# Lower words of the weights as integers into VectorE's product, their scale in the addition

## Chip, core and metric

One Trainium2 chip, of which the kernel uses one core. The time is device microseconds (us) of one launch. It was run three times: 1009.37, 1009.37 and 1008.32 us, median 1009.37. The names below: PE is TensorE (matmul), PEld its weight load, DVE is VectorE, ACT is ScalarE, POOL is GpSimd, SP is SyncE, which issues nearly all DMAs.

## What is computed

The reference is an attention with exponential features, whose result goes through a two-layer network with a cosine gate:

```python
def phi(x):                                   # x: (8, 8, 576, 64), w_phi: (64, 128)
    proj = np.einsum('bhsd,df->bhsf', x, w_phi)
    proj = proj - np.max(np.abs(proj), axis=-1, keepdims=True)
    return np.concatenate([np.exp(proj), np.exp(-proj)], axis=-1)
q_p, k_p = phi(q), phi(k)
kv = np.einsum('bhsf,bhsd->bhfd', k_p, v)
z = np.sum(k_p, axis=2)
num = np.einsum('bhsf,bhfd->bhsd', q_p, kv)
den = np.einsum('bhsf,bhf->bhs', q_p, z)[..., None] + 1e-06
x = num / den                                 # as 4608 tokens x 512
h = x @ w_in                                  # w_in: 512 x 2048
out = (h * np.cos(h)) @ w_out                 # w_out: 2048 x 512
```

`w_in` and `w_out` are drawn in 64-bit floats, and the kernel gets them as 64-bit words. For TensorE it splits each weight into two 32-bit floats, a high part and a remainder.

## The kernel before

**Two streams of work.** 32 units of attention (a unit is two heads of one batch) produce x, transposed, in a DRAM buffer `xs`; the network works on it in chunks of 512 tokens, in visits that take some of the eight pairs of w_in and w_out tiles each. The two streams run interleaved: attention ends near 680 us, and the network goes on to the end.

**Order.** Every piece of work is a `Step` with an engine, a function, the steps it depends on and the buffers it takes. `ORDER` (L88) is a list of all step numbers written out by hand; `plan()` (L260) follows it as it stands, and each engine runs its own steps in that order, one after the other. The costs given to a `Step` (0.4, 2.05, ...) are not used in placing anything. Waits between engines are derived from who reads and writes which buffer: a buffer is written anew when the last reader of its old contents is done.

**Weights.** `convert` (L368) is called for 16 tiles, w_in and w_out in turn (wi0, wo0, wi1, wo1, ...). Each loads 1 MB of 64-bit words into `w_raw`, of which there is one buffer (`w_raw=1` in `rings`, L285), so that the next tile's load has to wait until this one's last reader is done; the eight `f_raw` loads of `fold` (L501) use the same buffer afterwards. The scratch tiles `w_t0`, `w_t1`, `w_t2` exist once too. Per tile, `low` and `top` are the lower and upper 32-bit words, read with a step of 8 bytes (L386), and then:
- `scale`, ScalarE: L390 makes t0 from `top`; L391 converts `low` from unsigned integers into floats times 2^-52, in t2.
- `bits`, VectorE: L396, then L399 (reads `top`), then L402, which leaves in t1 the upper bits as a float and in t0 its power of two.
- `rest`, VectorE, L421: t2 = t2 x t0.
- `add`, VectorE, L435 (w_in) or L437 (w_out): the sum with t2. `high` (ScalarE, L50) and `low` (VectorE, L55) split the weight into two floats. For w_in `sums` follow (L445).
- `store`, SyncE, L455: the parts go to DRAM, from where `reload` (L491) fetches them later.

**SyncE's queue** issues its DMAs in `ORDER` as well: the weight loads (L378 for w_in, L381 for w_out), the heads of q and k (L554) and v (L558), the stores of x (L794, L798), the loads of x for the network (`x_raw<-xs`, L842; four per chunk), and the outputs. A DMA whose buffer isn't free yet holds up all that stand behind it. The load of wi1 is step 1295, and the product (`rest`) of wo0 before it is step 1289; in `ORDER` the load stands at place 207 and the product at place 239.

**Around the second weight load.** The four parts of x for the first chunk are loaded into `x_raw` (steps 1585 to 1588) and split by ScalarE into high parts (`xh_b<-x_raw` at L50; steps 1589, 1591, 1593, 1595), one for each load. In ScalarE's order step 1591 stands directly before the three copies of the q projection of attention unit 6 (L583 twice and L585, steps 251 to 253), from which VectorE takes the maxima (L589, step 254).

Of the kernel before, what the change touches and what calls it, by code (L numbers as in the profile page):

```python
# [7 lines left out]
F32 = mybir.dt.float32  # L8
# [3 lines left out]
AF = mybir.ActivationFunctionType  # L12
ALU = mybir.AluOpType
# [13 lines left out]
def phi_attention_then_cos_ffn(ctx: ExitStack, tc: tile.TileContext, qkT, vS, w_phi, w_in, w_out, out, out_t):  # L27
    nc = tc.nc
    PE, DVE, ACT, POOL, SP = nc.tensor, nc.vector, nc.scalar, nc.gpsimd, nc.sync
# [261 lines left out]
    def new(ring, shape, dtype, name, tag=None):  # L291

        pool = hot if ring in HOT else sb
        return pool.tile(shape, dtype, name=name, tag=tag or ring, bufs=rings[ring])
# [73 lines left out]
    def convert(kind, i):  # L368

        d = {}  # L370
        me = (kind, i)
        slot = w_slot[me] = w_buf(kind)
        name, eng, slow = ("POOL", POOL, 2.1) if me in W_POOL else ("DVE", DVE, 1.0)
# [10 lines left out]
        def scale():  # L384
            words = d["raw"].rearrange("p (n w) -> p n w", w=2)
            d["low"], d["top"] = words[:, :, 0], words[:, :, 1]  # L386
            d["t0"] = new("w_t", [P, 2 * DM], U32, f"{kind}_t0", "w_t0")
            d["t1"] = new("w_t", [P, 2 * DM], U32, f"{kind}_t1", "w_t1")
            d["t2"] = new("w_t", [P, 2 * DM], F32, f"{kind}_t2", "w_t2")
            ACT.activation(out=d["t0"].bitcast(F32), in_=d["top"].bitcast(F32), func=AF.Copy, scale=2.0 ** -112)  # L390
            ACT.activation(out=d["t2"], in_=d["low"], func=AF.Copy, scale=2.0 ** -52)  # L391

        def bits(k):
            t0, t1 = d["t0"], d["t1"]
            if k == 0:
                DVE.tensor_scalar(out=t0, in0=t0, scalar1=3, scalar2=0x7FFFFFFF, op0=ALU.logical_shift_left,  # L396
                                  op1=ALU.bitwise_and)
            elif k == 1:
                DVE.scalar_tensor_tensor(out=t1, in0=d["top"], scalar=0x80000000, in1=t0, op0=ALU.bitwise_and,  # L399
                                         op1=ALU.bitwise_or)  # L400
            else:
                DVE.tensor_scalar(out=t0, in0=t1, scalar1=0xFF800000, scalar2=None, op0=ALU.bitwise_and)  # L402

        def flat(x, first=0):

            return x.rearrange("p s f -> p (s f)") if kind == "wo" else x[:, first:first + 4].rearrange("p b (j c) -> p (b j) c", c=P)

        def whole(x):

            x = x.bitcast(F32)  # L410
            return x if kind == "wo" else x.rearrange("p (k s c) -> p s k c", k=4, s=2)

        def each(fn, out, *ins):
            if kind == "wo":
                fn(out, *ins)
                return
            o = out if len(out.shape) == 4 else out.rearrange("p (s k) c -> p s k c", s=2)
            fn(o, *[x if len(x.shape) == 4 else x.rearrange("p (s k) c -> p s k c", s=2) for x in ins])

        def rest():  # L420
            eng.tensor_tensor(out=d["t2"], in0=d["t2"], in1=d["t0"].bitcast(F32), op=ALU.mult)  # L421

        def high():
            d["w"] = w_tiles[me] = new(slot.ring, w_shape[kind], F32R, kind)
# [7 lines left out]

        def add():
            if kind == "wi":
                eng.tensor_tensor(out=d["t1"].bitcast(F32), in0=d["t1"].bitcast(F32), in1=d["t2"], op=ALU.add)  # L435
            else:
                each(lambda o, x, y: eng.tensor_tensor(out=o, in0=x, in1=y, op=ALU.add), flat(d["w"][:, 1]), whole(d["t0"]),  # L437
                     whole(d["t2"]))

        def sums(k):  # L440
            v = d["t1"].bitcast(F32).rearrange("p (h j s c) -> p h s j c", h=2, j=2, s=2)
# [14 lines left out]

        raw, t = Buf("w_raw"), Buf("w_t")
        s1 = Step("SP", 0.4, load, take=[raw], kind="w.load", pipe=3.0)
        s2 = Step("ACT", 2.05, scale, [s1], take=[t], use=[raw], kind="w.scale")
        last = s2  # L460
        for k, cost in enumerate((0.66, 1.22, 0.7)):
            last = s3 = Step("DVE", cost, lambda k=k: bits(k), [last], use=[t, raw] if k < 2 else [t], port=True, kind="w.bits")
        s5 = Step(name, 1.2 * slow, rest, [s3], use=[t], port=True, kind="w.rest")
        if kind == "wi":
            s7 = Step(name, 1.2 * slow, add, [s5], use=[t], port=True, kind="w.add")
            s4 = Step("ACT", 0.95, high, [s7], take=[slot], use=[t], kind="w.high")
            s7 = last = Step(name, 1.2 * slow, low, [s4, s7], use=[t, slot], port=True, kind="w.low")
            w_ready[me] = [s7]
            for k in range(4):
                last = Step(name, 0.425 * slow, lambda k=k: sums(k), [last], use=[t], port=True, kind="w.sums")  # L470
            s9 = Step("ACT", 0.95, sums_high, [last], use=[t, slot], kind="w.sums_high")
            s7 = Step(name, 1.2 * slow, sums_low, [s9], use=[t, slot], port=True, kind="w.sums_low")
        else:
            s4 = Step("ACT", 0.95, high, [s3], take=[slot], use=[t], kind="w.high")
            s6 = Step(name, 1.2 * slow, low, [s4, s5], use=[t, slot], port=True, kind="w.low")
            s7 = Step(name, 1.2 * slow, add, [s5, s6], use=[t, slot], port=True, kind="w.add")
            w_ready[me] = [s7]
# [1033 lines left out]
    for i in range(NP):  # L1511
        convert("wi", i)
        convert("wo", i)
# [83 lines left out]
```

## Time and profile before

| | |
|---|---|
| median of three runs | 1009.37 us |
| the profiled execution, its own time | 1007.43 us |
| its span (first to last instruction) | 1005.7 us |
| PE busy | 999.1 us (99%), 8970 matmuls |
| DVE busy | 864.4 us (86%), 1594 instructions |
| ACT busy | 809.1 us (80%), 1621 instructions |
| POOL busy | 175.8 us (17%) |
| HBM | 211 GB/s over the span |

The profiled execution took 1.7 us more than its span. Busy shares are means over the whole span. Matmuls are pipelined, so that one that waits can count as busy. The chain of work that ended last is followed backwards from the last instruction, at each step to what released it or to the instruction before it on the same engine.

### The profile page before, as it was taken

How to read it: one execution, taken by the hardware profiler on the slowest of the kernel's cores; microseconds unless marked ns; L12 is line 12 of the kernel's file. 1: busy time of each engine (PE TensorE's matmuls, PEld its weight loads, DVE VectorE, ACT ScalarE, POOL GpSimd, SP SyncE). 2: the span in 40 equal slices, each digit the busy share in tenths (PEclk: the TensorE clock that was granted, in tenths of full speed). 3: DMA queues.
4: the chain of work that ended last, by engine and by line, in shares of the span. 5: the costliest groups of instructions: out<-in, count | busy, mean ns of one | idle time of the engine just before them, and what ended most of it. 6: DMA issues, size and time to landing. Idle time of an engine off the chain costs nothing.

```text
span 1005.7 us, 22967 instructions
## 1 busy us (share of the span) xinstructions
PE 999.1 (99%) x8970; PEld 825.0 (82%) x8970; DVE 864.4 (86%) x1594; ACT 809.1 (80%) x1621; POOL 175.8 (17%) x231
## 2 busy tenths in 40 slices
PE   9999999999999999999999999999999999999998
PEld 7777877888888888889888898888888888888886
DVE  7999999999998987887778976699788998878885
ACT  6999999899979988989878998887566766665653
POOL 4544333201301113031132321120000000000000
PEclk9999999999999999999999999999999999999999
DMA  7575765566676766678876877465565574855274
GB/s 253 172 223 170 233 195 188 180 231 214 227 239 197 249 197 239 209 239 250 323 262 221 271 271 287 160 210 178 188 218 170 156 219 146 283 195 182 84 231 146
DMA packets 102620, 213.80 MB, mean 213 GB/s; under 512 B 21232, under 2 KB 52080, under 8 KB 98672
## 3 DMA queue, kind: packets, MB, share of 16 engines
q1 hardware_dynamic: 102368, 212.27, 63.7%
q8 instruction: 70, 1.15, 0.5%
q14 instruction: 38, 0.31, 0.1%
q10 hardware_dynamic: 144, 0.07, 0.0%
HBM read 155.68 MB, written 56.62 MB: 211 GB/s over the span
## 4 chain that ended last, share of the span: by engine, by line
PE 92%; DVE 5%; ACT 1%; DMA 1%; POOL 0%; issue 0%; SPq 0%; DVEq 0%; POOLq 0%; ACTq 0%
PE bank L1204 16%; PE bank L977 13%; PE bank L929 8%; PE bank L1026 7%; PE bank L1027 7%; PE bank L1028 7%; PE bank L757 5%; PE bank L1377 5%; PE bank L1379 5%; PE bank L1378 5%; PE bank L722 5%; PE bank L618 3%; PE bank L572 3%; PE bank L728 1%; DVE m L589 1%; PE bank L575 1%
## 5 line engine op out<-in xcount | busy, mean ns | idle before, releaser
L611 POOL TENSOR_TENSOR pq<-pq,bq 128x288 f32<-128x288 f32 x128 | 130.0, 1047 | 157.4 <-DVE bq L607 139.1
L676 ACT ACTIVATE ek<-bank,mk 128x128 f32<-128x128 f32 x464 | 128.1, 416 | 5.2 <-DVE mk L659 4.9
L1026 PE MATMUL bank<-wo,gh 128*128 128x512 f32 x320 | 128.6, 402 | 0.0
L1027 PE MATMUL bank<-wo,gh 128*128 128x512 f32 x320 | 125.1, 391 | 0.0
L1028 PE MATMUL bank<-wo,gl 128*128 128x512 f32 x320 | 125.0, 391 | 0.0
L603 POOL COPY m<-m 32x36 f32<-32x36 f32 x96 | 45.0, 469 | 341.6 <-DVE m L598 338.9
L1377 PE MATMUL bank<-gh,wo 128*128 128x512 f32 x224 | 87.7, 391 | 0.2 <-DVE o_t L1451 0.2
L1379 PE MATMUL bank<-gl,wo 128*128 128x512 f32 x224 | 87.5, 391 | 0.0
L1378 PE MATMUL bank<-gh,wo 128*128 128x512 f32 x224 | 87.4, 390 | 0.0
L682 ACT ACTIVATE eq<-pq 128x576 f32<-128x576 f32 x128 | 80.8, 706 | 1.5 <-POOL pq L611 1.1
L757 PEld LDWEIGHTS bank<-kv,eq 128*64 128x64 f32 x2048 | 64.3, 138 | 10.6 <-issue 3.3
L1026 PEld LDWEIGHTS bank<-wo,gh 128*128 128x128 f32 x320 | 60.2, 188 | 14.8 <-issue 2.2
L1028 PEld LDWEIGHTS bank<-wo,gl 128*128 128x128 f32 x320 | 60.1, 188 | 13.5 <-DVE gl L55 0.4
L757 PE MATMUL bank<-kv,eq 128*64 128x65 f32 x2048 | 70.0, 223 | 0.1
L1027 PEld LDWEIGHTS bank<-wo,gh 128*128 128x128 f32 x320 | 60.3, 188 | 10.1
L722 PEld LDWEIGHTS bank<-vs,ek 128*64 128x64 f32 x2048 | 62.5, 138 | 5.9 <-issue 2.2
L722 PE MATMUL bank<-vs,ek 128*64 128x65 f32 x2048 | 66.2, 223 | 0.0
L55 DVE TENSOR_TENSOR gl<-g,gh 128x512 fp32r<-128x512 f32 x80 | 58.1, 729 | 9.2 <-ACT gh L50 9.1
L1003 DVE SCALAR_TENSOR_TENSOR g<-g,hs 128x512 f32<-128x512 int32 x80 | 57.7, 725 | 8.9 <-ACT g L999 5.6
L1007 ACT ACTIVATE g<-g,halfpi 128x512 f32<-128x512 f32 x80 | 56.4, 719 | 10.2 <-DVE g L1003 9.5
L656 DVE TENSOR_REDUCE mk<-bank 128x4 f32<-128x512 f32 (+1 forms) x96 | 50.7, 542 | 15.9 <-PE bank L618 8.2
L1301 ACT ACTIVATE g<-hs 128x512 int32<-128x512 f32 x64 | 39.5, 628 | 29.8 <-DVE hs L1220 29.4
(184 smaller groups left out, 2623.3 us busy)
## 6 DMA issues: line engine op xcount, KB each, us to landing
wi<-wi_parts SPq DMA_DIRECT2D x22, 1792.0 KB, 8.6
qk<-qkT SPq DMA_DIRECT2D x31, 640.0 KB, 5.1
wo<-wo_sums SPq DMA_DIRECT2D x12, 1024.0 KB, 5.7
x_raw<-xs SPq DMA_DIRECT2D x47, 256.0 KB, 4.4
vs<-vS SPq DMA_DIRECT2D x32, 325.0 KB, 4.8
wo<-wo_parts SPq DMA_DIRECT2D x10, 1024.0 KB, 6.0
wi_raw<-w_in SPq DMA_DIRECT2D x8, 1024.0 KB, 7.1
wo_raw<-w_out SPq DMA_DIRECT2D x8, 1024.0 KB, 5.6
```

The lines of the kernel that those rows point to most:

```text
L611: qeng.tensor_tensor(out=d["pq"][:, c], in0=d["pq"][:, c], in1=d["bq"][:, c], op=ALU.subtract)
L676: ACT.activation(out=e[:, g, s * P:(s + 1) * P], in_=pk[:, g, :], func=AF.Exp, scale=1.0 - 2.0 * s, bias=d["lk" if s == 0 else "mk", i][:, ...
L722: PE.matmul(out=acc[c:c + 64, n, i, :], lhsT=e[:, s, P * n + c:P * n + c + 64], rhs=vs[b["v"].slot][:, 2 * s + i, :], start=(s == 0 and i ...
L757: PE.matmul(out=ps[64 * h:64 * h + 64, 65 * g:65 * g + 65], lhsT=d["eq", j][:, n, c:c + 64], rhs=d["kv"][:, 2 * n + j, :], start=h not in ...
L977: PE.matmul(out=bank(b), lhsT=w[:, part, 2 * r + kt // 2, kt % 2 * P:(kt % 2 + 1) * P], rhs=d.get(("from", kt), d)[x, kt], start=(k == 0), ...
L1026: PE.matmul(out=a, lhsT=gh[:, t], rhs=w[:, 0, r], start=first, stop=False)
L1027: PE.matmul(out=a, lhsT=gh[:, t], rhs=w[:, 1, r], start=False, stop=False)
L1028: PE.matmul(out=a, lhsT=gl[:, t], rhs=w[:, 0, r], start=False, stop=last)
L1204: PE.matmul(out=bank(bank_b), lhsT=w[:, part, block, j * P:(j + 1) * P], rhs=d[x, name, j], start=start and k == 0, stop=k == 5, skip_grou ...
L1377: PE.matmul(out=a, lhsT=w_of(0, m), rhs=n["gh"], start=first, stop=False, skip_group_check=True)
L1378: PE.matmul(out=a, lhsT=w_of(1, m), rhs=n["gh"], start=False, stop=False, skip_group_check=True)
L1379: PE.matmul(out=a, lhsT=w_of(0, m), rhs=n["gl"], start=False, stop=True, skip_group_check=True)
```

## The change

The instruction L391 of each of the 16 tiles is taken out of ScalarE's `scale`. VectorE's product reads the lower words from `w_raw` itself, as unsigned integers with a step of 8 bytes, and writes t2 without the factor 2^-52. The addition becomes a `scalar_tensor_tensor`, which multiplies t2 by 2^-52 and adds. `rest` is now a user of `w_raw`. `ORDER` stays as it is.

```diff
             ACT.activation(out=d["t0"].bitcast(F32), in_=d["top"].bitcast(F32), func=AF.Copy, scale=2.0 ** -112)
-            ACT.activation(out=d["t2"], in_=d["low"], func=AF.Copy, scale=2.0 ** -52)
...
         def rest():
-            eng.tensor_tensor(out=d["t2"], in0=d["t2"], in1=d["t0"].bitcast(F32), op=ALU.mult)
+            eng.tensor_tensor(out=d["t2"], in0=d["low"], in1=d["t0"].bitcast(F32), op=ALU.mult)
...
         def add():
             if kind == "wi":
-                eng.tensor_tensor(out=d["t1"].bitcast(F32), in0=d["t1"].bitcast(F32), in1=d["t2"], op=ALU.add)
+                eng.scalar_tensor_tensor(out=d["t1"].bitcast(F32), in0=d["t2"], scalar=2.0 ** -52, in1=d["t1"].bitcast(F32), op0=ALU.mult,
+                                         op1=ALU.add)
             else:
-                each(lambda o, x, y: eng.tensor_tensor(out=o, in0=x, in1=y, op=ALU.add), flat(d["w"][:, 1]), whole(d["t0"]),
-                     whole(d["t2"]))
+                each(lambda o, x, y: eng.scalar_tensor_tensor(out=o, in0=y, scalar=2.0 ** -52, in1=x, op0=ALU.mult, op1=ALU.add), flat(d["w"][:, 1]),
+                     whole(d["t0"]), whole(d["t2"]))
...
-        s2 = Step("ACT", 2.05, scale, [s1], take=[t], use=[raw], kind="w.scale")
+        s2 = Step("ACT", 1.02, scale, [s1], take=[t], use=[raw], kind="w.scale")
...
-        s5 = Step(name, 1.2 * slow, rest, [s3], use=[t], port=True, kind="w.rest")
+        s5 = Step(name, 1.2 * slow, rest, [s3], use=[t, raw], port=True, kind="w.rest")
```

## Rows read from the trace of the kernel before

**Rows 1.** The page of the profile: the busy time of each engine (part 1) and the chain of work that ended last by engine (part 4).

```profile
PE 999.1 (99%) x8970; PEld 825.0 (82%) x8970; DVE 864.4 (86%) x1594; ACT 809.1 (80%) x1621; POOL 175.8 (17%) x231
...
PE 92%; DVE 5%; ACT 1%; DMA 1%; POOL 0%; issue 0%; SPq 0%; DVEq 0%; POOLq 0%; ACTq 0%
```

**Rows 2.** The view by stretches. Columns: the stretch (us from the span's start), its length, then for PE, PEld, DVE, ACT and POOL the busy us with the number of instructions, the granted TensorE clock, the DMA share and GB/s.

```profile
40.00:60.00 20.00, 20.00 (x350) 14.81 (x344) 19.47 (x46) 19.45 (x40) 11.09 (x16) 1.00 0.76 241
...
80.00:100.00 20.00, 20.00 (x252) 15.35 (x250) 19.25 (x50) 19.73 (x36) 6.72 (x10) 1.00 0.54 158
...
120.00:160.00 40.00, 40.00 (x486) 31.80 (x486) 38.26 (x76) 39.88 (x86) 15.28 (x18) 1.00 0.60 186
```

**Rows 3.** The chain of work that ended last in order of time, from stretches 0 to 70 and 70 to 140 us. Columns: start us, us, what.

```profile
57.23 0.76 DVE m L589
...
64.33 1.16 PE bank L618 x16
...
106.04 1.57 DVE wo_t L421
```

**Rows 4.** Groups of instructions by line and shape. Columns: line, engine, operation, tiles, shapes, count | busy us, mean ns of one | idle us of the engine before them. First ScalarE, then VectorE.

```profile
L391 ACT ACTIVATE wi_t<-wi_raw 128x1024 f32<-128x1024 uint32 x8 | 9.4, 1176 | 0.0
...
L1003 DVE SCALAR_TENSOR_TENSOR g<-g,hs 128x512 f32<-128x512 int32 x80 | 57.7, 725 | 8.9 <-ACT g L999 5.6 <-ACT hs L985 3.1
L1010 DVE TENSOR_TENSOR g<-hs,g 128x512 f32<-128x512 f32 x80 | 57.1, 720 | 7.0 <-ACT g L1007 6.6
L399 DVE SCALAR_TENSOR_TENSOR wo_t<-wo_raw,wo_t 128x1024 uint32<-128x1024 uint32 x8 | 9.8, 1220 | 0.1
L421 DVE TENSOR_TENSOR wi_t<-wi_t,wi_t 128x1024 f32<-128x1024 f32 x8 | 9.7, 1218 | 0.1
```

**Rows 5.** The waits of the DMA queue of SyncE over the whole span. Columns: who waited for whom: us in total, times, the longest us.

```profile
SPq L378 <- DVE wo_t L399: 19.4, 5, 7.7
```

**Rows 6.** VectorE in order of time, around the second half of the first w_out tile. Columns: start us, us, engine, line, operation, tiles, count.

```profile
42.01 1.23 DVE L399 SCALAR_TENSOR_TENSOR wo_t<-wo_raw,wo_t 128x1024 uint32<-128x1024 uint32 x1
...
50.89 1.22 DVE L421 TENSOR_TENSOR wo_t<-wo_t,wo_t 128x1024 f32<-128x1024 f32 x1
...
57.23 0.76 DVE L589 TRANSPOSE_TENSOR_REDUCE m<-pq 128x18 f32<-128x576 f32 x1
```

**Rows 7.** SyncE in order of time in the same stretch: what it issues, and when.

```profile
43.31 0.38 SPq L378 DMA_DIRECT2D wi_raw<-w_in  x1
46.78 1.78 SPq L798 DMA_DIRECT2D xs<-xt  x4
48.60 2.21 SPq L842 DMA_DIRECT2D x_raw<-xs  x1
...
51.79 0.32 SPq L842 DMA_DIRECT2D x_raw<-xs  x1
...
52.63 0.91 SPq L558 DMA_DIRECT2D vs<-vS  x2
```

**Rows 8.** DMA issues of single moments. Columns: tiles, queue, operation, count, KB each, us from issue to landing. In this order: the x_raw load issued at 42.81, the w_in load at 43.31, the x_raw loads at 48.60 and 51.79, and the vs load at 52.63.

```profile
x_raw<-xs SPq DMA_DIRECT2D x1, 256.0 KB, 3.2
wi_raw<-w_in SPq DMA_DIRECT2D x1, 1024.0 KB, 7.2
x_raw<-xs SPq DMA_DIRECT2D x1, 256.0 KB, 5.3
x_raw<-xs SPq DMA_DIRECT2D x1, 256.0 KB, 4.4
vs<-vS SPq DMA_DIRECT2D x1, 325.0 KB, 4.7
```

**Rows 9.** ScalarE in order of time in the same stretch.

```profile
54.83 0.68 ACT L50 ACTIVATE xh_b<-x_raw 128x512 fp32r<-128x512 f32 x1
...
56.30 0.34 ACT L585 ACTIVATE pq<-bank 128x128 f32<-128x128 f32 x1
...
57.80 0.61 ACT L50 ACTIVATE xh_b<-x_raw 128x512 fp32r<-128x512 f32 x1
...
59.47 1.13 ACT L390 ACTIVATE wi_t<-wi_raw 128x1024 f32<-128x1024 f32 x1
```

**Rows 10.** TensorE in order of time in the same stretch; in brackets the idle us before an instruction and what ended it.

```profile
60.15 2.09 PE L722 MATMUL bank<-vs,ek 128*64 128x65 f32 x64
64.33 1.16 PE L618 MATMUL bank<-wphi,qk 64*128 64x128 f32 x16 [0.59 <-DVE rb L782]
```

**Rows 11.** Two later weight loads in order of time: the one at 100.64 with the product before it (VectorE) and the scaling that it feeds (ScalarE), and the one at 163.93 with the same.

```profile
100.64 0.38 SPq L378 DMA_DIRECT2D wi_raw<-w_in  x1
105.97 1.65 DVE L421 TENSOR_TENSOR wo_t<-wo_t,wo_t 128x1024 f32<-128x1024 f32 x1
119.52 1.27 ACT L390 ACTIVATE wi_t<-wi_raw 128x1024 f32<-128x1024 f32 x1
...
163.93 0.38 SPq L378 DMA_DIRECT2D wi_raw<-w_in  x1
166.41 1.21 DVE L421 TENSOR_TENSOR wo_t<-wo_t,wo_t 128x1024 f32<-128x1024 f32 x1
174.38 1.15 ACT L390 ACTIVATE wi_t<-wi_raw 128x1024 f32<-128x1024 f32 x1
wi_raw<-w_in SPq DMA_DIRECT2D x1, 1024.0 KB, 8.0
```

## The prediction, made before the changed kernel was run

> **What bounds the kernel now.** The page comes first: PE is busy 99% of the span, and the chain that ended last is 92% PE, 5% DVE and 1% ACT [rows 1]. That would say that nothing beside PE matters, but a matmul that waits counts as busy, so the chain in order of time is read next. It has two regimes. Up to 64 us it runs mostly over DVE; at 64.33 it goes to PE, whose first matmul there had waited for a DVE result [rows 3, 10]. Then it is PE almost without a break, but for a DVE stretch around 102 to 109 us (the product L421 at 106.04 stands in it [rows 3]). The view by stretches agrees: DVE is busy 19.47 of 20 us at 40 to 60 and 19.25 at 80 to 100, and ACT 19.45, 19.73 and, from 120 to 160, 39.88 of 40 [rows 2]. The granted clock is 1.00 in all of them. So before 64 us a microsecond of delay on DVE moves all that follows, and from about 110 us on only what starves PE counts. The weight tiles are converted from 10 to 370 us, over both regimes.
>
> **Instructions removed.** 16 conversions L391 go, of 1176 ns each [rows 4]: 16 x 1.176 = 18.8 us of ACT time. Only 1% of the chain is ACT, and the ACT chain pieces lie outside the weight conversions, so I price them at 0; the ends are 0 and what the second rival gives.
>
> **Instructions changed on DVE.** The addition becomes a `scalar_tensor_tensor`. Two such instructions stand beside plain products in the trace: L399, on 1024 elements, takes 1220 ns, and the product L421 1218 ns; L1003, on 512, takes 725 ns, L1010 720 ns [rows 4]. L399 already reads the words of `w_raw` with the step of 8 bytes, and L1003 already reads an integer operand beside a float. Nothing in the trace has both at once, or an unsigned operand that is converted on DVE. The ends: 0, and one further pass of 1.22 us per product if conversion and step together halve the rate. I take 0, the nearest rows, since each half is shown to be free; the other end is a rival.
>
> **The wait that is added.** This is the part with a cost. `w_raw` exists once. SP's queue already waits for the last reader, L399, in 5 of the w_in loads, 19.4 us in all [rows 5]. Now the last reader is L421. For wo0 L399 ends at 42.01 + 1.23 = 43.24, and the load of wi1 is issued at 43.31; L421 ends at 50.89 + 1.22 = 52.11 [rows 6, 7]. Nothing on DVE between them needs what SP issues after 43.31, so these instructions stay where they are, and the load goes out 0.07 after, at 52.18: **8.87 us later**. Behind it on SP stand the stores of x (46.78), the second x_raw load (48.60), a load of q and k, the third x_raw load (51.79) and two v loads (52.63) [rows 7].
>
> Who waits for these, the tightest first:
> - The x_raw load of 48.60 landed 5.3 us later, at 53.90 [rows 8]; ACT used it at 54.83 [rows 9]: 0.93 us of room. Its new issue is at best 52.18 + 0.44 + 1.82 = 54.44 (the weight load's issue and the four stores back to back, their lengths 0.38 and 1.78 plus small gaps [rows 7]), which is 5.84 later. At worst it keeps its distance from the weight load, 8.87 later: it took 2.21 us to issue, ending at 50.81, just after the weights had landed at 43.31 + 7.2 = 50.51 [rows 7, 8], which looks as if it had been held up by them. So ACT waits 5.84 - 0.93 = 4.9 to 8.87 - 0.93 = 7.9 us at 54.83.
> - Behind that instruction on ACT stand the copies of q for unit 6, the last of which ended at 56.64; DVE took it up at 57.23 [rows 9, 6]: 0.59 us of room. DVE starts its L589 **4.3 to 7.4 us late**, and nothing else can fill the gap, as its order is fixed.
> - That L589 at 57.23 is on the chain, and so is all up to PE's 64.33 [rows 3]; PE waited 0.59 us there for DVE [rows 10]. The delay goes through to PE in full, and from there on.
> - What is late next is covered: the v load goes from 52.63 to 58.5 or 61.5, lands 4.7 us later [rows 7, 8], and holds PE's L722 of 60.15 [rows 10] back by 3.0 to 6.0 us, less than the delay above. The third x_raw load is used at 57.80 [rows 9] and goes with the second. The weights of wi1 land at 52.18 + 7.2 = 59.4; their scaling stood at 59.47 [rows 8, 9] and is now later anyway.
>
> A floor for this term: the x_raw load issued at 54.44 lands as quickly as the one of 42.81, in 3.2 us [rows 8], at 57.64: ACT 2.8 and DVE 2.2 us late. I take the middle of 4.3 and 7.4, **5.8 us**.
>
> By the Trainium skill (DMA: Bandwidth & Descriptors, Queues, rings and completion order) each DMA engine takes the descriptors of one queue in the order of its ring, so that a load issued shortly after 1 MB of weights drains behind them. The trace agrees as far as it goes (5.3 us behind the weights, 3.2 without [rows 8]); by the rule alone the upper end, 7.4, would be the sum.
>
> **The other loads of weights.** The next pairs lie in the second regime. The load at 100.64 moves to the end of L421, 107.62, by 7.0 us; it would land some 7 us later, at about 115, and is used at 119.52 [rows 11]. The tightest is the load at 163.93: L421 ends at 167.62, the load comes 3.8 us later and, at 8.0 us, lands at 175.7, where ACT wanted it at 174.38 [rows 11], so ACT stands still for 1.3 us, and gives back 1.18 by the missing L391. PE has the chain there; I take 0, with 2 us as the end for all places together.
>
> **The sum.** Against the profiled execution: 1007.43 + 0 (ACT) + 0 (DVE) + 5.8 (SP's wait at 43.31) + 0 (other places) = 1013.2 us. That execution was 1.94 us below the median of the runs shown, so I forecast 1009.37 + 5.8 = **1015.2 us**; its own range is 1011.6 (the floor, 2.2) to 1018.8 (7.4 and the 2 us).
>
> **Rivals.**
> - The wait is hidden. The x_raw load could land early, or DVE and ACT could win back in the crowded stretch to 110 us what they lose: ACT's missing L391 gives it back 1.18 us a tile. For it: SP often stands idle, and PE looks busy all through. Against: 0.93 and 0.59 us of room on a chain of DVE. Time: 1009.4, give or take 2.
> - Faster: ACT is the true limit of the dense stretch. It is busy 19.73 of 20 us at 80 to 100 and 39.88 of 40 at 120 to 160, fuller than DVE in both [rows 2], and four conversions fall between 60 and 160. If each is worth its 1.18 us and the wait is hidden, the time is 1009.4 - 4.7 = 1004.7. It decides as soon as DVE or PE waits for ACT in that stretch for longer than ACT waits for DVE; against it stands the chain, with 1% of ACT. The Trainium skill (Perfetto Trace Analysis, Identifying the Most-Contended Engine) would have one shorten the engine with the highest occupancy first, which beside PE is ACT here; by that the change gains.
> - Slower by more: the strided unsigned product takes a second pass, 1.22 us. The four tiles that end before 111 us are on DVE's chain: 4 x 1.22 = 4.9 us on top, 1020.1. For it: no row has conversion and step at once; against: each is free by itself [rows 4].
>
> **Chances.** A difference of 0.2% (2 us) is about what a measurement of this kernel can tell from no change. Forecast 0.70, hidden wait 0.12, faster 0.10, second pass 0.08. Slower by over 0.2% (above 1011.4): nearly all of the first and the last, 0.76; within 0.2%: 0.14; faster: 0.10. The range 1009 to 1019.5 leaves out the faster case, half of the hidden one and the upper half of the last, some 0.2; the likeliest case's own stands above.
>
> **What would show it.** In the profile of the changed kernel: ACT has 1605 instructions instead of 1621; SP's waits name L421 where L399 stood, and the load of wi1 is issued near 52; ACT stands idle for 5 to 8 us before the high part of x near 55, with the x_raw load as the releaser; DVE stands idle for 4 to 7 us before L589; PE's matmul of 64.33 comes at 68.6 to 71.7, and the end is as much later. L421 and the additions take 1.22 us as before. I am wrong if the x_raw load at 48.60 is not later than 54, if ACT finds it landed, or if the delay of PE near 64 us is gone by 110.

## The result and the profile after

The changed kernel takes 1016.04 us (median of 6 runs, 1014.96 to 1018.13), and the kernel before, run beside it, 1008.76 (6 runs, 1008.17 to 1009.37): a ratio of 1.0070, 95% interval [1.0059, 1.0081]. It is slower by 7.3 us, where 5.8 were forecast. The profiled execution took 1016.21 us with a span of 1014.5, against 1007.43 and 1005.7.

The sum L435 of before is L434 now, the product L421 is L420, and L396, L399 and L402 are L395, L398 and L401; all other lines that are named kept their numbers.

The page of the changed kernel, parts 1 and 4, beside [rows 1]:

```profile
PE 1003.0 (99%) x8970; PEld 827.0 (82%) x8970; DVE 864.8 (85%) x1594; ACT 793.4 (78%) x1605; POOL 176.5 (17%) x231
...
PE 93%; DVE 4%; DMA 1%; ACT 1%; issue 0%; SPq 0%; POOL 0%; DVEq 0%; ACTq 0%; POOLq 0%
```

ACT has 16 instructions and 15.7 us less. DVE and PE have the same numbers of instructions and the same busy time within 0.4%. So hardly any work was added, and most of the 8.8 us of span must be waiting. The page does not say where: PE counts as busy for 99% as before.

The waits in SyncE's queue do (who waited for whom: us in total, times, the longest us), to be read against [rows 5]:

```profile
SPq L378 <- DVE wo_t L420: 51.9, 7, 11.7
...
SPq L381 <- DVE wi_t L420: 32.8, 5, 8.9
```

L378 waited 19.4 us for L399 before; it now waits 51.9 us for L420, at most 11.7 us at once. The loads of w_out, L381, had this row before:

```profile
SPq L381 <- DVE wi_t L399: 20.4, 5, 7.3
```

Together 84.7 us of waiting where there were 39.8, and the page of the engines shows none of it. The first of these waits stands in SyncE's order of time (start us, us, line, tiles, count), beside [rows 7]:

```profile
52.98 0.38 SPq L378 DMA_DIRECT2D wi_raw<-w_in  x1
53.41 2.29 SPq L798 DMA_DIRECT2D xs<-xt  x4
55.75 0.43 SPq L842 DMA_DIRECT2D x_raw<-xs  x1
56.28 0.38 SPq L554 DMA_DIRECT2D qk<-qkT  x1
60.85 0.32 SPq L842 DMA_DIRECT2D x_raw<-xs  x1
```

The load of wi1 goes out at 52.98 instead of 43.31, and with it all that stands behind: the stores of x, the second x_raw load at 55.75 instead of 48.60, a load of q and k at 56.28 instead of 50.91, the third x_raw load at 60.85 instead of 51.79, the v loads at 61.69 instead of 52.63. What it waited for, and what waited in the end, stands in VectorE's order of time, beside [rows 6] (in brackets the idle time before an instruction and what ended it):

```profile
51.68 1.22 DVE L420 TENSOR_TENSOR wo_t<-wo_raw,wo_t 128x1024 f32<-128x1024 uint32 x1
...
63.07 0.78 DVE L589 TRANSPOSE_TENSOR_REDUCE m<-pq 128x18 f32<-128x576 f32 x1 [4.97 <-ACT pq L585]
```

L420 ends at 52.90, and the load follows 0.08 later. L589, at 57.23 before, starts at 63.07, and VectorE had stood still for 4.97 us. Between the two lies ScalarE, beside [rows 9]:

```profile
61.27 0.63 ACT L50 ACTIVATE xh_b<-x_raw 128x512 fp32r<-128x512 f32 x1 [5.50 <-DMA x_raw<-xs]
```

It waited 5.50 us for the x_raw load, whose time to landing is given in the view of DMA issues, beside [rows 8]; in this order the weights, that x_raw load and the load of q and k behind it:

```profile
wi_raw<-w_in SPq DMA_DIRECT2D x1, 1024.0 KB, 5.8
...
x_raw<-xs SPq DMA_DIRECT2D x1, 256.0 KB, 5.5
...
qk<-qkT SPq DMA_DIRECT2D x1, 640.0 KB, 6.6
```

TensorE follows, beside [rows 10]; its instruction of 64.33 is now at 70.83:

```profile
62.97 0.77 PE L643 MATMUL bank<-wphi,qk 128*128 128x128 f32 x2 [4.09 <-ACT pq L583]
63.53 3.62 PE L664 MATMUL bank<-mk,minus 128*128 128x512 f32 x4
...
70.83 1.06 PE L618 MATMUL bank<-wphi,qk 64*128 64x128 f32 x16
```

L643 reads q and k. Their load landed at 56.28 + 6.6 = 62.9 us, just ahead of it. So the x_raw load isn't alone in holding up TensorE: had it come in time, TensorE would have waited for q and k here nearly as long; load_between, below, is such a case.

And the chain that ended last, which has DVE's L589 of 57.23 in [rows 3], now goes through the second x_raw load to TensorE:

```profile
55.75 5.50 DMA x_raw<-xs
...
61.90 0.98 ACT pq L583 x2
...
62.97 0.77 PE bank L643 x2
```

The groups of VectorE's instructions that the change touches (count | busy us, mean ns of one | idle us before), beside [rows 4]:

```profile
L420 DVE TENSOR_TENSOR wo_t<-wo_raw,wo_t 128x1024 f32<-128x1024 uint32 x8 | 10.8, 1351 | 0.1
L434 DVE SCALAR_TENSOR_TENSOR wi_t<-wi_t,wi_t 128x1024 f32<-128x1024 f32 x8 | 9.8, 1221 | 0.1
L420 DVE TENSOR_TENSOR wi_t<-wi_raw,wi_t 128x1024 f32<-128x1024 uint32 x8 | 9.8, 1219 | 0.0
L437 DVE SCALAR_TENSOR_TENSOR wo<-wo_t,wo_t 128x1024 fp32r<-128x1024 f32 x8 | 9.7, 1212 | 0.1
```

The product of a w_in tile takes 1219 ns with the strided unsigned operand and took 1218 without it; that of a w_out tile takes 1351 (1348 before), and the two forms of the addition 1221 and 1212. The new instructions cost what the old ones did.

### The profile page after: what moved, and what is told of

Same layout as the page of the kernel before. It is cut to its first block, busy times and chain, and to the rows that moved or that the text cites. A ratio compares the mean times of both kernels' runs of the same rounds, so it can differ in the third digit from the quotient of the medians.

```text
span 1014.5 us, 22946 instructions
## 1 busy us (share of the span) xinstructions
PE 1003.0 (99%) x8970; PEld 827.0 (82%) x8970; DVE 864.8 (85%) x1594; ACT 793.4 (78%) x1605; POOL 176.5 (17%) x231
## 4 chain that ended last, share of the span: by engine, by line
PE 93%; DVE 4%; DMA 1%; ACT 1%; issue 0%; SPq 0%; POOL 0%; DVEq 0%; ACTq 0%; POOLq 0%
PE bank L1204 15%; PE bank L977 12%; PE bank L929 8%; PE bank L1026 7%; PE bank L1027 7%; PE bank L1028 7%; PE bank L757 6%; PE bank L722 5%; PE bank L1377 5%; PE bank L1379 5%; PE bank L1378 5%; PE bank L572 3%; PE bank L618 3%; PE bank L728 1%; PE bank L643 1%; PE bank L664 1%
## 5 line engine op out<-in xcount | busy, mean ns | idle before, releaser
L611 POOL TENSOR_TENSOR pq<-pq,bq 128x288 f32<-128x288 f32 x128 | 129.9, 1045 | 156.3 <-DVE bq L607 141.1
L1007 ACT ACTIVATE g<-g,halfpi 128x512 f32<-128x512 f32 x80 | 56.7, 720 | 12.8 <-DVE g L1003 12.0
L1003 DVE SCALAR_TENSOR_TENSOR g<-g,hs 128x512 f32<-128x512 int32 x80 | 57.8, 726 | 8.5 <-ACT g L999 5.6
L1010 DVE TENSOR_TENSOR g<-hs,g 128x512 f32<-128x512 f32 x80 | 57.7, 728 | 7.8 <-ACT g L1007 7.4
```

Of the source, the lines that this page charges most:

```text
L611: qeng.tensor_tensor(out=d["pq"][:, c], in0=d["pq"][:, c], in1=d["bq"][:, c], op=ALU.subtract)
```

## Where the time goes from there: a table of shifts

To see what becomes of a delay, one takes the same instruction in two traces and subtracts the starts. The table does this with transposes of the maxima (L607 on VectorE), of which one stands at 52.70 us in the kernel before, directly ahead of the place in question. Profiles differ there already, by -0.2 to 1.1 us, in kernels that ought to be equal up to then, so this first difference is taken off each row. A number is thus the us by which a kernel, in its one profiled execution, has fallen behind since 52.70. The execution of before that it is held against was 1.3 us under the median of its runs, so late columns are uncertain by about 1 us; the last row, of a kernel whose runs equal those of before, shows how much.

| at (us, time of before) | 62 | 101 | 270 | 320 | 349 | 379 |
|---|---|---|---|---|---|---|
| the changed kernel | 4.96 | 5.54 | 5.64 | 6.50 | 7.93 | 7.12 |
| act_back | 5.18 | 5.14 | 5.79 | 7.04 | 8.52 | 7.71 |
| wo0_only | 5.13 | 5.10 | 5.20 | 5.16 | 5.16 | 5.16 |
| all_but_wo0 | 0.00 | -0.02 | 0.45 | 1.53 | 2.88 | 2.06 |
| load_after_x | 0.00 | 0.28 | 1.01 | 1.21 | 2.81 | 2.00 |
| two_loads_after | 0.00 | 0.61 | 1.25 | 1.22 | 1.22 | 1.22 |
| load_between | 1.07 | 3.44 | 3.54 | 3.79 | 5.17 | 4.35 |
| all_loads_after | 0.00 | -0.04 | -0.48 | 0.37 | 0.20 | -0.33 |
| before_all_loads_after | 0.00 | 0.58 | 0.77 | 1.79 | 1.63 | 1.30 |

The first row: 4.96 of 7.12 us arise at once, at 62. Some 2.3 more come between 270 and 349, where nothing was forecast, and 0.8 are regained by 379. (By 645 us the changed kernel stands at 8.1; what happens there is told at the end of the part on the prediction.) The other rows are experiments, told now. In the diffs a number stands for a step of `ORDER`, and `...` for what is left out.

## Experiments

### One tile, and all the others

**wo0_only** is the kernel before with the change made for the tile wo0 alone, the one whose product holds up the load of wi1; **all_but_wo0** has the change for the other 15. The diff is against the changed kernel; in all_but_wo0 the first line has `!=`. The addition is switched in the same way, which the cut leaves out.

```diff
+        ints = me == ("wo", 0)
...
+            if not ints:
+                ACT.activation(out=d["t2"], in_=d["low"], func=AF.Copy, scale=2.0 ** -52)
...
-            eng.tensor_tensor(out=d["t2"], in0=d["low"], in1=d["t0"].bitcast(F32), op=ALU.mult)
+            eng.tensor_tensor(out=d["t2"], in0=d["low"] if ints else d["t2"], in1=d["t0"].bitcast(F32), op=ALU.mult)
...
-        s5 = Step(name, 1.2 * slow, rest, [s3], use=[t, raw], port=True, kind="w.rest")
+        s5 = Step(name, 1.2 * slow, rest, [s3], use=[t, raw] if ints else [t], port=True, kind="w.rest")
```

> The change made for one of the 16 weight tiles alone, the first w_out tile (wo0), whose product now holds up the load of wi1. Theory 1, the wait in SyncE's queue: this tile carries most of the loss, 5.0 to 6.5 us over the kernel before (about 1013.8 to 1015.3 us against 1008.8), and ScalarE stands idle 5 to 6 us for an x_raw load shortly before the high part of x near 55 us. Theory 2, the cost lies in the changed instructions or in the missing ScalarE instruction, alike in all tiles: a sixteenth of 7.3 us, 0.5 us or less, no difference to be seen.

> The change made for the 15 other tiles, wo0 as before. Theory 1, the wait: what is left is the later places, of which the profile of the changed kernel shows one, the load of wo7 near 340 us, which held up a load of partial sums: 0 to 2.5 us over the kernel before, and no idle ScalarE near 55 us. Theory 2, alike in all tiles: 15/16 of 7.3 us, 6.8 us over.

wo0_only: 1013.88 us against 1008.96, ratio 1.0054 [1.0038, 1.0070]. all_but_wo0: 1010.01, ratio 1.0006 [0.9991, 1.0022]. ScalarE's split of the second part of x, first in wo0_only, then in all_but_wo0:

```profile
60.62 0.63 ACT L50 ACTIVATE xh_b<-x_raw 128x512 fp32r<-128x512 f32 x1 [5.67 <-DMA x_raw<-xs]
```

```profile
54.67 0.68 ACT L50 ACTIVATE xh_b<-x_raw 128x512 fp32r<-128x512 f32 x1
```

One tile makes ScalarE wait for 5.67 us and the kernel some 4.9 us slower; the fifteen others make it 1.05 slower, which the interval does not tell from nothing. In the trace of the fifteen, though, 2.88 us are lost by 349 (2.06 by 379), and the chain there goes through a DMA (start us, us, what):

```profile
335.33 6.00 DMA o<-sums
341.42 0.70 DVE o L1073
```

`o<-sums` fetches the running sum of the network's output, to which L1073 (L1066 in the kernel before) adds a new part.

### The load moved behind the x loads

**load_after_x** is the changed kernel with the step of wi1's load, 1295, moved in `ORDER` from place 207 to directly behind the third x_raw load, 1587. Nothing else differs. If the queue's order is the cause, its price for wi1 has to go.

```diff
-        178, 82, 1585, 208, 222, 190, 121, 228, 1295, 226, 264, ...
+        178, 82, 1585, 208, 222, 190, 121, 228, 226, 264, ...
...
-        ... 196, 270, 1290, 225, 1587, 232, 1289, ...
+        ... 196, 270, 1290, 225, 1587, 1295, 232, 1289, ...
```

> The changed kernel with one step moved in SyncE's order: the load of wi1 stands behind the third x_raw load of the first chunk (step 1587) instead of ahead of the stores before it. It still waits for the product of wo0, but holds up no x_raw load. Theory 1, the wait: 0 to 2.5 us over the kernel before, as with the 15 tiles; ScalarE takes the high part of x near 55 us without a wait. Theory 2, the instructions: stays at 7 us over, since all of them are still there. Theory 3, it is the lateness of the wi1 words themselves: stays at 5 us or more over, since they come no earlier.

1010.02 us, ratio 1.0019 [1.0008, 1.0030], where the changed kernel had 1016.04 and 1.0070: 6.0 us less by the medians, 5.1 by the ratios. ScalarE no longer waits:

```profile
54.94 0.67 ACT L50 ACTIVATE xh_b<-x_raw 128x512 fp32r<-128x512 f32 x1
```

The delay at 62 us is 0.00 in the table. So the cost at this place was the loads of x, q and k held up behind a weight load, not the product or the addition, and not the later arrival of the weights: these were loaded at 52.29 here too. What is left, 2.00 us at 379, is about that of all_but_wo0 (2.06).

**load_between** moves the step only behind the second x_raw load, 1586 (`193, 195, 1586, 1295, 215`), so that the load of q and k (step 215), the third x_raw load and the v loads stand behind the weights.

> The changed kernel with the load of wi1 moved between the second x_raw load (step 1586) and the load of q and k that follows it, so that of the DMAs of the first chunk only the third x_raw load, that load of q and k and the v loads are held up. If the second x_raw load alone sets the stall near 55 us, as the prediction's steps say: ScalarE takes the high part near 55 us on time; the third x_raw load goes out near 52.6, lands 4.4 us later and is wanted at 57.8, so the stall there is 0 to 1 us; in all 0 to 3.5 us over the kernel before (1009 to 1012.5). If the third x_raw load or the v loads had set it: 4 us or more over.

1012.09 us, ratio 1.0036 [1.0024, 1.0047]. The second part of x is on time, but the third one holds ScalarE, and the load of q and k holds TensorE:

```profile
55.96 0.68 ACT L50 ACTIVATE xh_b<-x_raw 128x512 fp32r<-128x512 f32 x1
...
62.26 0.63 ACT L50 ACTIVATE xh_b<-x_raw 128x512 fp32r<-128x512 f32 x1 [3.23 <-DMA x_raw<-xs]
```

```profile
61.85 0.77 PE L636 MATMUL bank<-wphi,qk 128*128 128x128 f32 x2 [2.63 <-DMA qk<-qkT]
62.41 3.28 PE L657 MATMUL bank<-mk,minus 128*128 128x512 f32 x4
```

ScalarE's wait of 3.23 us is more than the 0 to 1 us that was expected of it: I had taken 4.4 us to landing for the third x_raw load, as in [rows 8], and here it took 7.8, issued 1.13 us behind the weights (54.45 against 53.32) and right behind the 640 KB of q and k:

```profile
wi_raw<-w_in SPq DMA_DIRECT2D x1, 1024.0 KB, 5.3
...
x_raw<-xs SPq DMA_DIRECT2D x1, 256.0 KB, 7.8
```

It is not this wait that the kernel pays for, though. The chain that ended last does not go through ScalarE here; it goes through the load of q and k to TensorE's L636 (L643 in the kernel before) and on from there:

```profile
53.80 7.91 DMA qk<-qkT
```

VectorE is then 1.07 us behind at 62, after 0.96 us of waiting for L636, while TensorE comes to L611 (L618 in the kernel before) 3.6 us late, with the 1.14 us by which this trace is late at 52.70 taken off, which is about what the table has at 101 (3.44). That TensorE loses more than the 2.63 us of its wait is taken up in the last section.

### The second place

**two_loads_after** moves the load of the last w_out tile, wo7 (step 1494), as well, to directly behind step 1473, the fetch of the running sum at which the chain showed the later loss.

```diff
-        ... 2152, 1473, 1987, ...
+        ... 2152, 1473, 1494, 1987, ...
```

> The changed kernel with two loads moved behind what they hold up: wi1 as before, and wo7 (near 333 us) behind the partial sums that the next chunk needs. If the wait of wo7 costs the 1.4 us by which VectorE falls back near 340 us in the trace of the changed kernel and of the run with wi1 alone moved: about 1 us under that run (1010.0), within 1.5 us of the kernel before. If that shift is made up later anyway: no different from the run with wi1 alone moved, 2 us over.

1009.34 us, ratio 1.0004 [0.9995, 1.0013]. Between 320 and 349 us load_after_x loses 1.60 us and this kernel 0.00. By 379 load_after_x has regained 0.8 of that, so that 0.8 us last; the medians differ by 0.7, and the two intervals overlap. VectorE's addition there (L1059) has no wait any more:

```profile
339.78 0.68 DVE L1059 TENSOR_TENSOR o<-bank,o 128x512 f32<-128x512 f32 x1
```

How that place works is seen in the two kernels of the result. The kernel before, SyncE, then VectorE, then the DMA issue of 330.08 (KB, us to landing):

```profile
327.37 0.38 SPq L381 DMA_DIRECT2D wo_raw<-w_out  x1
...
330.08 0.38 SPq L1061 DMA_DIRECT2D o<-sums  x1
```

```profile
338.71 0.68 DVE L1066 TENSOR_TENSOR o<-bank,o 128x512 f32<-128x512 f32 x1
```

```profile
o<-sums SPq DMA_DIRECT2D x1, 256.0 KB, 3.6
```

The changed kernel, the chain, and then VectorE:

```profile
340.26 0.38 SPq L381
...
341.25 6.09 DMA o<-sums
```

```profile
347.43 0.69 DVE L1066 TENSOR_TENSOR o<-bank,o 128x512 f32<-128x512 f32 x1 [1.35 <-DMA o<-sums]
```

Before, the sum was there at 330.08 + 3.6 = 333.7, 5.0 us before it was wanted. In the changed kernel all is 7.3 us later by then (6.50 and the 0.79 taken off the table); the fetch at 341.25 is another 3.9 us late, since the load of wo7 in front of it waited for L420, and its 6.1 us to landing, behind that load, are 2.5 more. 3.9 + 2.5 - 5.0 = 1.4, and VectorE waits 1.35 us.

**all_loads_after** moves the loads of all ten tiles for which a place behind the next urgent DMA was found (1295, 1325, 1374, 1385, 1404, 1415, 1434, 1464, 1475 and 1494), and **before_all_loads_after** is the kernel before with the same `ORDER`, as a control: it shows what the moves alone are worth.

> The changed kernel with ten of the weight loads moved behind the DMAs that they hold up (wi1, wi2, wo3, wi4, wo4, wi5, wo5, wo6, wi7, wo7). Theory 1, the wait: no loss is left, within 1 us of the kernel before (1007.8 to 1009.8). If the ScalarE time that is saved were worth something by itself, it would show here as a gain, up to 4.7 us (1004). Theory 2, the instructions: 7 us over.

> The kernel before with the same ten weight loads moved as in the run with ten loads moved (control). If moving loads does nothing by itself there: within 1 us of the kernel before, and the run with ten loads moved, which has 16 ScalarE conversions fewer, shows what these are worth: 0 to 1 us. If the waits for L399 in SyncE's queue cost the kernel before something too: 1 to 3 us faster than it.

1008.66 us, ratio 1.0002 [0.9992, 1.0012], and 1008.82 us, ratio 0.9995 [0.9985, 1.0004]. SyncE still waits for the product in all_loads_after, 45.0 us in all, but nothing urgent stands behind the waiting loads any more. So the change costs nothing then, and the 16 ScalarE instructions that it saves gain nothing either, both to within the 1 us of the intervals.

### The instruction put back

**act_back** is the changed kernel with L391 put back; what it writes is overwritten by the product, so it adds only ScalarE's time.

```diff
             ACT.activation(out=d["t0"].bitcast(F32), in_=d["top"].bitcast(F32), func=AF.Copy, scale=2.0 ** -112)
+            ACT.activation(out=d["t2"], in_=d["low"], func=AF.Copy, scale=2.0 ** -52)
```

> The changed kernel with the 16 ScalarE conversions L391 put back in their old place; their result is overwritten by the product and not used, so that only their time is added. If the ScalarE time that the change saves is worth nothing, as the chain of before says: the same as the changed kernel, 1015 to 1017 us. If it gives back a part of the loss (1.2 us in each of the first tiles): up to 4.7 us slower than the changed kernel, 1020 us.

1016.23 us, ratio 1.0069 [1.0055, 1.0083]; the changed kernel had 1.0070. ScalarE waits as there:

```profile
61.02 0.63 ACT L50 ACTIVATE xh_b<-x_raw 128x512 fp32r<-128x512 f32 x1 [5.73 <-DMA x_raw<-xs]
```

So no gain from the missing instruction can be seen behind the wait either, to within the 1.4 us of the interval.

### The product put forward

Instead of moving the load back, the reader can be moved forward. **product_early_wo0** puts the third step of `bits` and the product of wo0 directly behind the second step of `bits` in VectorE's order; **product_early** does so for all 16 tiles.

```diff
-        173, 172, 187, 1286, 174, 175, 1287, 118, ...
+        173, 172, 187, 1286, 174, 175, 1287, 1288, 1289, 118, ...
```

At their old places 1288 and 1289 are taken out.

> The changed kernel with VectorE's order changed for wo0 alone: its masking (L401) and product (L420) stand directly behind the instruction L398 that reads the upper words, so that w_raw is free some 2 us after it instead of 9. SyncE's order is as it was. Wait theory: the load of wi1 goes out near 45.2 instead of 52.2, the second x_raw load is 0 to 1.9 us late, of which 0.9 us are covered, so ScalarE near 55 us waits 0 to 1 us; the later places stay: 0 to 3.5 us over the kernel before (1009 to 1012.5). Rival: VectorE is so full there that 1.9 us of work put forward delay what others wait for by as much, and nothing is won: 6 us over or more.

> The same for all 16 tiles: the product directly behind the instructions before it. Wait theory: all waits but about 2 us each go, also the one of wo7 near 333 us; within 2 us of the kernel before (1007.5 to 1011). Rival, as in the run with wo0 alone: what is put forward delays the gating of the network (L1003, L1010) and the attention's maxima, 3 us over or more.

product_early_wo0: 1011.57 us against 1008.61, ratio 1.0029 [1.0020, 1.0039]. The load goes out at 45.97, and ScalarE does not wait for x, but its split of x comes at 57.48, 2.65 us later than before (this trace is 0.67 us late already ahead of the two instructions). ScalarE waits 3.15 us for VectorE ahead of 46.34, where the kernel before has a wait of 0.36 ahead of 43.69. VectorE's order is tight there, and the two instructions put forward delay what stands behind them. product_early: 1024.47 us, ratio 1.0156 [1.0124, 1.0188], far worse than the change itself, where 1007.5 to 1011 was expected if the waits alone counted. Its profiled execution is the shortest of its four, 1020.61 us. ScalarE's longest waits between 170 and 370 us, in product_early (its L1000, L996 and L977 are the L1007, L1003 and L984 of before), and in the kernel before:

```profile
ACT g L1000 <- DVE g L996: 11.6, 8, 3.8
ACT g L977 <- DVE gl L55: 7.5, 5, 3.5
```

```profile
ACT g L1007 <- DVE g L1003: 7.2, 8, 1.8
...
ACT g L984 <- DVE gl L55: 2.1, 6, 0.5
```

There ScalarE waits for VectorE's part of the cosine gate, 19.1 us where it was 9.3. In the kernel before the chain of this stretch is TensorE's, and yet the stretch does not bear some 2 us of conversion per tile at another point of VectorE's order.

None of these kernels beats the one before; all_loads_after and before_all_loads_after equal it.

## Why the prediction was right, and where it was not

- **Instructions removed, 0.** Right to within 1 to 2 us: act_back, and all_loads_after beside its control. The rival by which ScalarE is the true limit has fallen, though it was busy for 39.88 of 40 us [rows 2]: in that stretch VectorE waited 1.2 us for it, and no matmul of TensorE did.
- **Instructions changed on DVE, 0.** Right: 1219 and 1221 ns, no second pass, and that rival has fallen with them.
- **The added wait: the load of wi1 8.87 us later.** Right in each link that is priced. With the 0.79 us taken off by which this trace is late at its start, the load went out at 52.19, where 52.18 was worked out. The x_raw load came at 54.96, 0.5 later than the best case (the four stores took 2.29 us instead of 1.78), and landed 5.5 us after. ScalarE stood still for 5.50 us (4.9 to 7.9), VectorE for 4.97 (4.3 to 7.4, taken 5.8).
- **The size taken, 5.8.** A little too much, and the reason of its upper end was wrong. The prediction took it that the weights ahead had held up the x_raw load of 48.60, in its 2.21 us of issue and its 5.3 us to landing. The same load has nearly the same times in load_after_x, where the weights stand behind it, and shorter ones in all_but_wo0, where they stand ahead of it as before (first load_after_x, then all_but_wo0):

```profile
48.79 2.06 SPq L835 DMA_DIRECT2D x_raw<-xs  x1
...
x_raw<-xs SPq DMA_DIRECT2D x1, 256.0 KB, 5.5
```

```profile
48.45 0.45 SPq L849 DMA_DIRECT2D x_raw<-xs  x1
...
x_raw<-xs SPq DMA_DIRECT2D x1, 256.0 KB, 3.6
```

  So there was no distance of 5.29 us to keep: in the changed kernel the x_raw load waited in the queue only for the weight load's issue and the stores, followed at 2.77 us and took 5.5 us again. By the Trainium skill (DMA: Bandwidth & Descriptors, Queues, rings and completion order) each DMA engine consumes the descriptors of one ring in their order. That 1 MB of weights ahead makes this load land later is not shown by these rows; what they show is that it is issued later.
- **It goes through to PE in full and stays.** Right: wo0_only keeps 5.1 us from 62 to 379, and the rival in which the wait is hidden has fallen. The floor, an x_raw load that lands in 3.2 us, was not reached.
- **What is late next is covered.** Right for the v load and the third x_raw load. But the load of q and k, which the prediction lists behind the weights, was not asked for its room at all. In the changed kernel it landed 0.1 us ahead of TensorE's use; when load_between let the second x_raw load pass, it held TensorE for 2.63 us.
- **The other loads of weights, 0, with 2 us as the end.** This step failed in its reason, and its size was a little low. all_but_wo0 lost 2.06 us by 379 in its trace, and 1.05 by the medians, where the interval allows 0. The prediction asked of each load only when its weights land and are wanted, and named the load at 163.93 as the tightest. The changed kernel lost 0.10 us from 101 to 270, so that load cost next to nothing. The price arose where another DMA stood behind the weight load, as with wi1: at wo7, by the fetch of the running sum, with 1.6 us in the traces, of which 0.8 last. The smaller losses between 270 and 320 us (0.86 in the changed kernel) were not traced to a load, and are near what two profiles differ by.
- **The clock, for which there was no term.** The prediction read a granted clock of 1.00 and put nothing for what a standstill of TensorE does to it. Of the six executions of the changed kernel, the two with a mean clock of 1.000 and 0.998 took 1014.96 and 1015.02 us, the four with 0.996 and 0.997 took 1015.86 to 1018.13. Of the nine of load_between, five with 0.999 and 1.000 took 1010.38 to 1012.09, four with 0.998 took 1012.43 to 1014.65; of the four of product_early, 1020.61 (1.000), 1022.87 (0.998), 1026.07 (0.997) and 1028.37 (0.995). The two of the changed kernel with the higher clock are 6.2 to 6.3 us above the kernel before. So an estimate from these numbers is that some 1 us of the 7.3 goes with the clock; that the clock is its cause, and not a longer wait the cause of both, is not shown.
- **The sum.** The trace of the changed kernel has 4.96 for wi1 and 2.16 for the rest by 379, together 7.1; the medians of wo0_only and all_but_wo0 have 4.9 and 1.05, together 6.0, with intervals of some 1.5 us to either side of each. Measured were 7.3, and the forecast had 5.8 and 0. That the other places cost something is therefore shown by the traces and by two_loads_after, and their size only to 1 to 2 us. That the total came within 1.5 us is in part luck, since 0.8 too much for wi1 made up for some of what was left out; and the 1015.2 us lie nearer still to the 1016.04 because the 1009.37 they start from, a median of three, were 0.6 above that of six.

What stays open: single profiles differ between 574 and 650 us by up to 3.8 us, also in kernels that are equal there. The largest such loss, in wo0_only, begins with a gap in TensorE's own stream, inside the 16 matmuls of L625 (L618 in the kernel before), for which the chain names no releaser:

```profile
592.25 1.79 issue
```

Behind it the granted clock was 0.68 from 595 to 600 us. Why TensorE stopped there is not known.

## What to carry to other kernels

When an edit lets a later instruction be the last reader of a buffer, look up the DMA that refills the buffer and then everything that stands behind it in the issuing queue: what that DMA itself brings is often early enough, and what stands behind it is not. Where the order is written out by hand, such an edit has to move the DMA in it too; moving one list entry gave back 5 to 6 of 7.3 us here. And a full engine is no limit by that alone: 16 instructions of 1.18 us taken from an engine that was busy for 99.7% of a stretch changed nothing that could be measured.

## What was not expected of the hardware

The granted clock fell. The view by stretches of the changed kernel (PE, PEld, DVE, ACT and POOL busy us with counts, granted clock, DMA share, GB/s), beside [rows 2]:

```profile
60.00:65.00 5.00, 2.03 (x4) 1.26 (x5) 1.93 (x3) 3.73 (x8) 0.00 (x0) 0.60 0.74 234
65.00:70.00 5.00, 5.00 (x77) 3.09 (x77) 4.54 (x14) 3.18 (x6) 1.30 (x4) 0.72 0.68 224
```

TensorE stood still for 4.09 us before 62.97, and then the clock was 0.60 on the mean from 60 to 65 us, between its two levels (1.2 and 2.4 GHz), 0.72 up to 70 and 1.00 again from there; the kernel before has 1.00 in both stretches. The four matmuls of L664 took 3.62 us (the row of 63.53 above), those at the same place of the kernel before half of that:

```profile
58.34 1.88 PE L664 MATMUL bank<-mk,minus 128*128 128x512 f32 x4
```

What this cost differs from kernel to kernel. The changed kernel fell back by 0.58 us more between 62 and 101; wo0_only, with 0.73 from 60 to 65 and 0.93 up to 70, by none, and act_back, with 0.83 in both, by none. In these VectorE was 5.0 to 5.2 us behind by then, more than the 4.1 to 4.3 us that TensorE had waited, so that TensorE had time to lose. In load_between VectorE was only 1.07 us behind. The clock there was 0.68 from 60 to 65:

```profile
60.00:65.00 5.00, 3.15 (x6) 1.60 (x6) 3.59 (x11) 2.74 (x4) 1.04 (x3) 0.68 0.93 336
```

The four matmuls took 3.28 us instead of 1.88. With the same 1.14 us taken off, TensorE was 2.7 us late at L636 and 3.6 late at L611, in front of which the kernel before has 0.59 us of idle time to give away [rows 10]. At full clock 2.7 - 0.59 = 2.1 would have been left, so an estimate from these numbers is that the clock cost 1.5 us there. So a wait that starves TensorE can cost twice, once as a wait and once by the clock behind it, if TensorE is what the rest then waits for; in the trace of the changed kernel the second part was at most 0.6 us up to 101.
